# A windowed-attention plus mixture-of-experts kernel: weight loads moved earlier, conversions respaced, the last scatter halved

## The chip, the core and the metric

The kernel runs on one core of a Trainium2 chip. The metric is device time in microseconds (us) of one execution; several executions are timed, and one more is recorded by the hardware profiler. Engines are named as in the profile: PE (TensorE; PEld is its weight load), DVE (VectorE), ACT (ScalarE), POOL (GpSimd), SP (SyncE, which here only issues DMAs). A "q" behind a name (SPq, DVEq) is the engine's sequencer.

## The reference, cut to what matters

```python
# q, k, v: (8 batches, 8 heads, 576, 64); causal attention over a window of 64
scores = where(0 <= i - j < 64, q @ k.T / 8, -1e9)
x = (softmax(scores) @ v), heads joined          # (4608 tokens, 512)
do = x @ w_skip > 0
e = argmax(x @ w_gate); gate = softmax(x @ w_gate)[e]      # 8 experts
out = x;  out[do] = x + gate * (relu(x @ w1[e]) @ w2[e])   # w1: 512x1024, w2: 1024x512
```

## The kernel before

**First half, attention.** 36 tiles of 128 tokens are made in a software pipeline written out by hand: in step `t` the loop issues the loads of later steps (`at`), `score(t + 1)`, the gate products (`gate_at`), the softmax of tile `t` (`lessen`, `raise_e`), the output product of tile `t - 2` (`tile_out`, which calls `av_tile`), and the transposes of tile `t - 1`. Each engine runs its instructions in the order in which the code issues them, with semaphore waits between engines. `av_tile` writes the result of a tile to `x`, a pool of four buffers (`XPB`), and `store` sends it to `out`, at most three tiles behind. So tile 29 writes the buffer that the store of tile 25 must have left. All these loads and stores are issued by SP, one after the other, on SP's one queue.

**Routing, beside it.** POOL and DVE find each token's expert and its place in a list. After tile 21 POOL ranks the experts once (`close_first`) and writes `perm`, the row numbers of the first two experts' weights. SP reads `perm` into a register (L843, TENSOR_LOAD) before it can issue the first weight load. The lists of the last tiles are made after the attention, in generators that are stepped beside the first expert products (`late`, `later`, `side`).

**Second half, experts.** Ten items (an expert's tokens, up to 400) go through four quarters each. A quarter `k` is an up product of piece `(k, 0)` and, two quarters later, a down product of piece `(k - 2, 1)`. A piece is 128x1024 float32, 512 KB: loaded to a `raw` buffer (L845; the attention loop loads the first six, one at each step that `U0` names), then split for PE into `whi` (ACT, L854) and `wlo` (DVE, L858). `weights_to(n)` splits until `n` pieces are done; `expert_chunk` calls it ahead of each chunk of PE work and chooses `n`. Hidden activations are split likewise (`hh` on ACT L991, `hl` on DVE L994).

**The end.** An item's result `yo` is scattered to `out` by an indirect DMA that POOL issues (`give`, L1031). The last item has 112 rows, one token tile; its last quarter is made in two column halves, `z` = 0 and 1, each with its own DVE instruction (L1082). Behind it stands a conditional block for left-over tokens, skipped here: every engine loads the count `left` into a register (`left_over`, L1026) and branches (L1465). In the instruction streams the last DVE instruction (`z` = 1) and the last scatter stand behind that branch.

Of the kernel before, what the change touches and what calls it, by code (L numbers as in the profile page):

```python
# [11 lines left out]
I32 = mybir.dt.int32  # L12
AF = mybir.ActivationFunctionType
ALU = mybir.AluOpType
# [5 lines left out]
N, D, E, F = 4608, 512, 8, 1024  # L20
P = 128
# [31 lines left out]

NSLOW = 4
NRAW, NEARLY = 6, 2
U0 = (29, 30, 31, 32, 33, 34)
RATE = 1

BOTH = 20
# [7 lines left out]
PAIRED = 160  # L67
# [76 lines left out]
def window_attention_moe(ctx: ExitStack, tc, a, out):  # L144
    nc = tc.nc
# [570 lines left out]
    side, pace = [], [None]  # L716
# [14 lines left out]
    def rows_apart(ins):  # L731
        tc.declare_no_dep(ins.ins, group="rows", reason="every token is in one list entry: rows are disjoint")
        tc.add_to_no_dep_group("rows", ins.ins)
# [22 lines left out]
    OTHERS = [e for e in mybir.ALL_ENGINES if e != PE]  # L756

    GRP = [8, 8, 6, 6, 8]
    late = []

    later = []
# [48 lines left out]
    part = lambda k, w: (ITEMS[steps[k][0]][2], steps[k][1], w)  # L810
# [7 lines left out]
    when = {pc: n for n, pc in enumerate(pieces)}  # L818
# [16 lines left out]
    ptr = {"dma": 0, "split": 0, "free": 0, "use": 0}  # L835
# [13 lines left out]
    def weight_dma_first():  # L849
        weight_dma(ptr["dma"])  # L850
        ptr["dma"] += 1
# [10 lines left out]
    def weight_split(n):  # L862
        weight_hi(n)
        weight_lo(n, nc.vector)

    def weights_to(n):
        n = min(n, len(pieces), ptr["free"] + len(ring))
        while ptr["split"] < n:
            while ptr["dma"] < len(pieces) and idle:
                if not can_load(ptr["dma"]):  # L870
                    break
                weight_dma(ptr["dma"])
                ptr["dma"] += 1
            if ptr["dma"] == ptr["split"]:
                break
            weight_split(ptr["split"])
            ptr["split"] += 1
        while ptr["dma"] < len(pieces) and idle and can_load(ptr["dma"]):
            weight_dma(ptr["dma"])
            ptr["dma"] += 1  # L880
# [3 lines left out]
    def can_load(n):  # L884
        return pieces[n][0] % E < 2 or "order" in tables
# [139 lines left out]
    def left_over(engines):  # L1025
        return nc.values_load(tables["left"][0:1, 0:1], engines=engines, min_val=0, max_val=NSLOT)  # L1026

    counts = []

    def give(idx, yo):  # L1030
        ins = nc.gpsimd.indirect_dma_start(  # L1031
            out=out,
            out_offset=bass.IndirectOffsetOnAxis(ap=idx, axis=0),
            in_=yo,
            in_offset=None,
            bounds_check=N - 1,
            oob_is_err=False,
        )
        rows_apart(ins)
# [19 lines left out]
    def down(it, qi, wh, wl, tags="u"):  # L1059
        hh, hl = it.hh[qi], it.hl[qi]  # L1060
        if qi == 0:
            it.ys = []
            for tag in tags:
                for _ in range(1 if tag == "u" else 2):
                    pool = banks["v" if tag == "v" else "late"]
                    y = pool.tile([P, D], F32, name="y" + tag, tag=tag, bufs=1 if tag == "u" else 2)
                    it.ys.append(y)
        if it is its[-1]:
            m, ending_q = it.n, qi == NQ - 1
            halves = [(f, z) for f in range(2) for z in range(2)]  # L1070
            if ending_q:
                halves.sort(key=lambda fz: fz[1])
                yo = hpool["y"].tile([P, D], F32, name="yo", bufs=3)[:m]
            for f, z in halves:
                y = it.ys[z][:m, 0 : D // 2]
                w = slice(f * D + z * D // 2, f * D + (z + 1) * D // 2)
                mm3(y, hh[:, f], hl[:, f], wh[:, w], wl[:, w], qi == 0 and f == 0, ending_q and f == 1)
                if ending_q and f == 1:
                    if z == 1:
                        counts.append(left_over(OTHERS))  # L1080
                    c = slice(z * D // 2, (z + 1) * D // 2)
                    nc.vector.scalar_tensor_tensor(  # L1082
                        yo[:, c], y, it.gate[0], it.xg[0][:m, c], op0=ALU.mult, op1=ALU.add
                    )
                elif not ending_q and z == 1:
                    yield 0.65
            if ending_q:
                give(it.idx[0], yo)
            return
        for f in range(2):  # L1090
            w = slice(f * D, (f + 1) * D)
            first, last = qi == 0 and f == 0, qi == NQ - 1 and f == 1
            for j, y in enumerate(it.ys):
                m = it.rows[j]
                if it.small and j == it.nt - 1:
                    if f == 1:
                        down_small(it, qi, y, m)
                    continue
                r = slice(j * P, j * P + m)
                mm3(y[:m], hh[:, f, r], hl[:, f, r], wh[:, w], wl[:, w], first, last)  # L1100
            yield 0.65 * it.nt
        if qi == NQ - 1:

            def end():
                for j, y in enumerate(it.ys):
                    finish(y, it.xg[j], it.idx[j], it.gate[j], it.small and j == it.nt - 1)
                xfree.extend(it.xg)
                if it is its[-3]:
                    nc.gpsimd.drain()

            ending.append(end)
# [54 lines left out]
    with tc.manual_schedule():  # L1166
# [31 lines left out]
        for m in range(B // 2):  # L1198
            z = 2 * (m == 0)
# [9 lines left out]
        for t in range(NT - 1):  # L1209
            m, r = divmod(t, 9)  # L1210
# [37 lines left out]
            for f, n, j in lower_at.get(t, ()):  # L1248
                f(n, j)
            for _ in range(U0.count(t)):  # L1250
                weight_dma_first()
# [34 lines left out]
        place, turn = [0], [0, 0]  # L1286
# [4 lines left out]
        def expert_chunk():  # L1291
            k = place[0]
            last = len(steps) - 1
            if k != turn[0]:
                turn[:] = k, 0
            need = max(when[part(min(k + 1, last), 0)], when[part(min(k - 1, last), 1)] if k else 0) + 1
            most = ptr["free"] + min(RING, len(ring)) - 1
            it = its[steps[min(k, last)][0]]
            if late or later or side or P < it.n <= PAIRED:
                calm = k > 0 and turn[1] in ((1, 2) if k > 1 else (1,))  # L1300
                if turn[1] < 3:
                    need = max(when[part(min(k, last), 0)], when[part(k - 2, 1)] if k > 1 else 0) + 1
                weights_to(max(need, min(ptr["split"] + calm, most)))
            else:
                weights_to(max(need, min(ptr["split"] + RATE, most)))
            turn[1] += 1
            place[0], c = next(chunks)

        expert_chunk()
        drip()  # L1310
        tile_out(NT - 1)
# [12 lines left out]
        mr = moe.enter_context(tc.tile_pool(name="mr", bufs=1, side="right", reuse_waits="tile"))  # L1324
# [122 lines left out]
        while True:  # L1447
            k = place[0]
# [16 lines left out]
    with tc.If(more > 0):  # L1465
        with tc.For_i(0, more, 1) as i:
# [11 lines left out]
            it = Item(P)  # L1478
# [3 lines left out]
            for qi in range(NQ):  # L1482
                both = []
                for w in range(2):
                    n = 2 * qi + w
# [57 lines left out]
```

## Time and profile before

| | us |
|---|---|
| timed runs (3) | 402.59 to 403.35, median 402.61 |
| profiled execution, its own time | 404.55 |
| span of the profiled execution, first to last instruction | 402.8 |
| PE busy | 390.5 |
| DVE busy | 304.3 |
| mean granted TensorE clock | 0.995 of full speed |

The span is what the trace's times count from. The profiled execution took 1.94 us longer than the median of the timed ones, and 1.75 us lie around its span. Attention ends near 157 us; the lists are made until about 189 us; from there on PE runs expert products to 396.8 us.

### The profile page before, as it was taken

Reading aid. Unit: us, or ns where it says so; the run is one execution under the profiler, and the core shown is the slowest. Engines: PE = TensorE matmul, PEld = TensorE weight load, DVE = VectorE, ACT = ScalarE, POOL = GpSimd, SP = SyncE. Lnnn points to the kernel's source line nnn. Section 1 sums busy time; section 2 is a strip of 40 time slices with the busy share of each in tenths; the row PEclk is TensorE's granted clock in tenths of the full one; section 3 lists DMA queues with packets and bytes.
Section 4 is the critical chain, followed back from the end, with each engine's and each line's share of the span. In section 5 each row is a group of like instructions: output and inputs, shape, how many; then the busy total and the mean of one; then the engine's idle time right before and its main releaser. Section 6 shows DMA issues by size and latency. Waiting matters only on the chain.

```text
span 402.8 us, 11515 instructions
## 1 busy us (share of the span) xinstructions
PE 390.5 (97%) x4642; PEld 327.4 (81%) x4642; DVE 304.3 (76%) x538; ACT 218.1 (54%) x372; POOL 156.2 (39%) x276
## 2 busy tenths in 40 slices
PE   8999999999999999989999999999999999999994
PEld 3787778877787788878888888998888889988883
DVE  2888799899989898997758799465456485668981
ACT  1778776866876795554333554244335355444450
POOL 5121368157558688873605033032026030100410
PEclk9999999999999999999999999999999999999998
DMA  8999999999995887745705968645136787643420
GB/s 295 406 399 404 405 409 407 409 391 376 393 336 168 293 293 210 277 158 180 233 2 177 303 242 271 196 166 176 54 130 212 231 279 254 206 164 106 133 105 23
DMA packets 34600, 99.41 MB, mean 247 GB/s; under 512 B 4368, under 2 KB 5648, under 8 KB 34544
## 3 DMA queue, kind: packets, MB, share of 16 engines
q1 hardware_dynamic: 30480, 87.30, 61.5%
q0 software_dynamic: 3200, 9.58, 6.8%
q10 hardware_dynamic: 864, 1.77, 1.2%
q8 instruction: 37, 0.61, 0.6%
q14 instruction: 19, 0.16, 0.1%
HBM read 84.57 MB, written 14.39 MB: 246 GB/s over the span
## 4 chain that ended last, share of the span: by engine, by line
PE 59%; issue 14%; DVE 13%; DMA 7%; ACT 4%; POOL 2%; POOLq 0%; SPq 0%; DVEq 0%; ACTq 0%
PE av L388 7%; PE p L928 5%; PE pt L281 5%; PE p L930 5%; PE p L929 5%; PE ps L252 4%; DMA out<-yo,les 4%; DVE s L268 3%; PE yv L928 3%; PE yv L929 3%; PE yv L930 3%; DVE mx L267 2%; PE pw L331 2%; DMA raw<-wq 2%; PE ps L238 2%
## 5 line engine op out<-in xcount | busy, mean ns | idle before, releaser
L858 DVE TENSOR_TENSOR wlo<-raw,whi 128x1024 fp32r<-128x1024 f32 x70 | 85.6, 1237 | 13.5 <-ACT whi L854 11.7
L1031 POOL DMA_INDIRECT out<-yo,les x18 | 20.1, 1116 | 141.2 <-DVE yo L1022 132.4
L991 ACT ACTIVATE hh<-p 128x256 fp32r<-128x256 f32 (+4 forms) x56 | 22.9, 409 | 95.6 <-PE p L930 86.9
L854 ACT CAST whi<-raw 128x1024 fp32r<-128x1024 f32 x72 | 73.8, 1046 | 0.0
L928 PE MATMUL p<-xp,whi 128*128 128x256 f32 (+4 forms) x192 | 58.2, 303 | 0.2 <-ACT xp L902 0.2
L929 PE MATMUL p<-xp,whi 128*128 128x256 f32 (+4 forms) x192 | 57.1, 297 | 0.2 <-DVE xp L905 0.2
L994 DVE SCALAR_TENSOR_TENSOR hl<-p,hh 128x256 fp32r<-128x256 f32 (+4 forms) x56 | 25.0, 450 | 42.4 <-ACT hh L991 26.6
L930 PE MATMUL p<-xp,wlo 128*128 128x256 f32 (+4 forms) x192 | 56.9, 297 | 0.1
L273 ACT ACTIVATE s<-s 128x1024 f32<-128x1024 f32 x36 | 38.1, 1058 | 28.0 <-DVE s L268 27.6
L267 DVE TENSOR_REDUCE mx<-ps 128x8 f32<-128x1024 f32 x36 | 43.6, 1211 | 6.7 <-PE ps L252 6.7
L268 DVE TENSOR_TENSOR s<-ps,mx 128x1024 f32<-128x1024 f32 x36 | 44.1, 1225 | 4.6
L388 PEld LDWEIGHTS av<-vm,ptm 128*64 128x64 f32 x992 | 34.4, 136 | 8.9 <-issue 5.9
L388 PE MATMUL av<-vm,ptm 128*64 128x74 f32 x992 | 39.2, 230 | 0.1
L281 PE MATMUL pt<-gid,s 128*128 128x128 f32 x280 | 38.4, 279 | 0.1
L928 PEld LDWEIGHTS p<-xp,whi 128*128 128x128 f32 x192 | 36.2, 188 | 2.7 <-issue 0.6
L282 ACT COPY ptm<-pt 128x512 f32<-128x512 f32 x70 | 37.3, 581 | 1.2 <-PE pt L281 0.8
L929 PEld LDWEIGHTS p<-xp,whi 128*128 128x128 f32 x192 | 36.2, 188 | 1.2 <-DVE xp L905 0.5
L930 PEld LDWEIGHTS p<-xp,wlo 128*128 128x128 f32 x192 | 36.2, 188 | 0.3 <-DVE wlo L858 0.3
L252 PE MATMUL ps<-k,q 64*64 64x128 f32 x1024 | 33.4, 269 | 0.0
L281 PEld LDWEIGHTS pt<-gid,s 128*128 128x128 f32 x280 | 30.1, 141 | 3.1 <-issue 0.4
L353 POOL COPY vm<-vm 64x1184 f32<-64x1184 f32 (+1 forms) x17 | 18.8, 1108 | 35.4 <-ACT vm L351 23.8
L252 PEld LDWEIGHTS ps<-k,q 64*64 64x64 f32 x1024 | 30.2, 133 | 2.1
(241 smaller groups left out, 827.4 us busy)
## 6 DMA issues: line engine op xcount, KB each, us to landing
raw<-wq SPq DMA_DIRECT2D x72, 512.0 KB
vm<-vp SPq DMA_DIRECT2D x16, 592.0 KB
vT<-vT SPq DMA_DIRECT2D x16, 512.0 KB
out<-x SPq DMA_DIRECT2D x32, 256.0 KB
q<-qT SPq DMA_DIRECT2D x13, 512.0 KB
k<-kT SPq DMA_DIRECT2D x8, 640.0 KB
k<-kT SPq DMA_DIRECT2D x7, 512.0 KB
kt<-kT SPq DMA_DIRECT2D x8, 256.0 KB
```

The costliest lines, as they stand in the source:

```text
L252: nc.tensor.matmul(ps[64 * hf : 64 * hf + 64, r, p], q[h, p], k[h, :, p], start=False, stop=p == 3, skip_group_check=True,)
L267: nc.vector.tensor_reduce(mx, flat, axis=AX.X, op=ALU.max)
L268: pace[0] = nc.vector.tensor_tensor(s, flat, mx.unsqueeze(2).to_broadcast([P, 8, P]), op=ALU.subtract)
L273: nc.scalar.activation(s, s, AF.Exp, scale=0.125)
L281: nc.tensor.transpose(pt[:, p], s[:, 4 * r + p], ident)
L282: nc.scalar.copy(ptm[:, 4 * r : 4 * r + 4], pt)
L388: nc.tensor.matmul(av[64 * hf : 64 * hf + 64, h // 4, (h % 4) * VW : (h % 4 + 1) * VW], ptm[:, (h % 2) * 4 + h // 2, 64 * hf : 64 * hf + 6 ...
L854: nc.scalar.copy(ring[n % RING][0], raw_of[n])
L858: by.tensor_tensor(lo, raw_of[n], hi.bitcast(F32), op=ALU.subtract)
L928: nc.tensor.matmul(o, lh, rh, start=first, stop=False, skip_group_check=parts)
L929: nc.tensor.matmul(o, lh, rl, start=False, stop=False, skip_group_check=parts)
L930: nc.tensor.matmul(o, ll, rh, start=False, stop=last, skip_group_check=parts)
```

## The change

Four edits. `U0`: the six first weight pieces are issued at steps 28, 29, 30, 30, 31, 31 in place of 29 to 34. `expert_chunk`: while lists are made, a split is allowed at every second chunk, ahead of what is needed by one piece, and no further than the next need. `left_over` on the engines other than PE is called ahead of the last quarter's down product. The last result goes out in two scatters of half rows: `out` is seen as 9216 rows of 256, with indices `2 * idx + z` that two small DVE instructions write.

```diff
-U0 = (29, 30, 31, 32, 33, 34)
+U0 = (28, 29, 30, 30, 31, 31)
...
-    def give(idx, yo):
+    def give(idx, yo, parts=1):
         ins = nc.gpsimd.indirect_dma_start(
-            out=out,
+            out=out.rearrange("n (z c) -> (n z) c", z=parts),
...
+            if ending_q:
+                counts.append(left_over(OTHERS))
+                half = mr.tile([P, 2], I32, name="half")
+                for z in range(2):
+                    nc.vector.tensor_scalar(
+                        half[:m, z : z + 1], it.idx[0], 2.0, float(z), op0=ALU.mult, op1=ALU.add
+                    )
...
                 if ending_q and f == 1:
-                    if z == 1:
-                        counts.append(left_over(OTHERS))
                     c = slice(z * D // 2, (z + 1) * D // 2)
                     nc.vector.scalar_tensor_tensor(
                         yo[:, c], y, it.gate[0], it.xg[0][:m, c], op0=ALU.mult, op1=ALU.add
                     )
+                    give(half[:m, z : z + 1], yo[:, c], 2)
...
-            if ending_q:
-                give(it.idx[0], yo)
...
-            if late or later or side or P < it.n <= PAIRED:
-                calm = k > 0 and turn[1] in ((1, 2) if k > 1 else (1,))
-                if turn[1] < 3:
-                    need = max(when[part(min(k, last), 0)], when[part(k - 2, 1)] if k > 1 else 0) + 1
-                weights_to(max(need, min(ptr["split"] + calm, most)))
+            now = max(when[part(min(k, last), 0)], when[part(k - 2, 1)] if k > 1 else 0) + 1
+            if late or later or side:
+                calm = turn[1] % 2 == (0 if k > 1 else 1)
+                weights_to(max(now, min(need, ptr["split"] + calm)))
+            elif P < it.n <= PAIRED:
+                weights_to(max(now if turn[1] < 3 else need, min(ptr["split"] + (turn[1] in (1, 2)), most)))
```

How the order of instructions changes, at three places (`-` before, `+` after):

On SP, at attention steps 28 and 29: `vT`, `vm`, `vTt` and `vt` are the last value loads of the attention, `out<-x` is the store of tile 25, `raw` the weight pieces.

```order
 L211 DMA q<-qT 128x1024
 L426 DMA out<-x 128x512
+L843 TENSOR_LOAD perm
+L843 ISA x2
+L845 ISA
+L845 DMA raw_123<-wq 128x1024
 L292 DMA vT<-vT 128x1024
 L298 DMA vm<-vp 128x2x592
```

The register load of `perm` and the first weight piece now stand ahead of those four loads and that store; before they stood directly behind them. Two more pieces each now stand ahead of the loads of `kt` and `qt` (step 31) and of the store of tile 28 (step 32).

On DVE, in the stretch where the last lists are made (L604 is the one-hot table of the last tiles, L994 the low part of the hidden activations, L858 the low part of a weight piece):

```order
 L905 TENSOR_TENSOR xp_3348<-px_3518,xp_3348 128x4x128
-L994 SCALAR_TENSOR_TENSOR hl<-p_3525,hh 128x256
 L858 TENSOR_TENSOR wlo_3353<-raw_123,whi_3352 128x1024
+L994 SCALAR_TENSOR_TENSOR hl<-p_3528,hh 128x256
 L604 TENSOR_TENSOR xg_122<-cf,gk 128x1024
 L858 TENSOR_TENSOR wlo_3355<-raw_124,whi_3354 128x1024
 L994 SCALAR_TENSOR_TENSOR hl<-p_3578,hh 128x256
-L994 SCALAR_TENSOR_TENSOR hl<-p_3593,hh 128x256
 L858 TENSOR_TENSOR wlo_3357<-raw_125,whi_3356 128x1024
+L994 SCALAR_TENSOR_TENSOR hl<-p_3606,hh 128x256
```

A weight conversion now stands ahead of an `hl` where it stood behind it; ACT's `whi` and `hh` change places in the same way, and the number of conversions is the same.

On POOL, at the end of the program, of the change alone (`half` are the indices of the half rows; the ISA with eight waits closes the skipped block):

```order
L1026 TENSOR_LOAD left_4429 [waits DVE_49]
L1031 DMA out<-yo_5868,half_5865 9216x256 [waits DMASW3_49,DVE_49]
L1470 COMPARE_AND_BRANCH
...
L1470 ISA [waits DMASW4_49,DMASW5_49,DMASW3_49,DMASW6_49,DMASW2_49,DMASW7_49,DMASW1_49,DMASW0_49]
L1470 UNCONDITIONAL_BRANCH
L1031 DMA out<-yo_5868,half_5865 9216x256 [waits DMASW4_49,DVE_49]
```

The scatter of half 0 stands ahead of the branch and that of half 1 behind it; between them is the ISA that waits for the completion of POOL's own DMAs on all eight of their semaphores. It stood there before too, with both halves' one scatter behind it.

## Rows read from the trace of the kernel before

**Rows 1.** Page, parts 1, 2 (40 slices) and 5 (the conversions on ACT).

```profile
PE 390.5 (97%) x4642; PEld 327.4 (81%) x4642; DVE 304.3 (76%) x538; ACT 218.1 (54%) x372; POOL 156.2 (39%) x276
...
GB/s 295 406 399 404 405 409 407 409 391 376 393 336 168 293 293 210 277 158 180 233 2 177 303 242 271 196 166 176 54 130 212 231 279 254 206 164 106 133 105 23
...
L854 ACT CAST whi<-raw 128x1024 fp32r<-128x1024 f32 x72 | 73.8, 1046 | 0.0
```

**Rows 2.** Timeline of SP, 108 to 185 us: start, duration, issue.

```profile
116.54 0.34 SPq L426 DMA_DIRECT2D out<-x  x1
118.02 0.33 SPq L292 DMA_DIRECT2D vT<-vT  x1
...
123.40 0.38 SPq L426 DMA_DIRECT2D out<-x  x1
129.79 0.36 SPq L845 DMA_DIRECT2D raw<-wq  x1
130.26 0.91 SPq L428 DMA_DIRECT2D out<-x  x1
```

**Rows 3.** Timeline of POOL, 98 to 200 us: what writes perm.

```profile
128.53 0.23 POOL L653 TENSOR_SCALAR perm<-cm 128x2 int32<-128x2 f32 x1
```

**Rows 4.** Timeline of PE, 108 to 200 us: attention step 31.

```profile
133.52 0.64 PE L331 MATMUL pw<-vT,gid 128*32 128x256 f32 x8
```

**Rows 5.** Timeline of DVE, 108 to 200 us: x of tile 29.

```profile
136.34 0.69 DVE L401 TENSOR_TENSOR x<-av,r 128x512 f32<-128x512 f32 x1
```

**Rows 6.** Windows: busy time by engine, granted clock, DMA share, GB/s.

```profile
130.00:131.00 1.00, 1.00 (x30) 0.91 (x30) 0.87 (x2) 0.72 (x2) 0.94 (x2) 1.00 0.13 49
131.00:134.00 3.00, 3.00 (x64) 2.18 (x59) 2.80 (x7) 2.50 (x4) 2.66 (x5) 1.00 0.84 255
137.00:141.00 4.00, 4.00 (x90) 3.20 (x86) 3.80 (x10) 2.62 (x6) 2.78 (x12) 1.00 1.02 368
399.00:401.00 2.00, 0.00 (x0) 0.00 (x0) 0.00 (x0) 0.00 (x0) 0.12 (x1) 0.50 0.32 99
```

**Rows 7.** Timeline of PE, 176 to 200 us: its one long wait.

```profile
180.84 0.50 PE L929 MATMUL yw<-wlo,hh 128*128 128x512 f32 x1 [1.21 <-DVE wlo L858]
```

**Rows 8.** Timeline of DVE, 108 to 200 us: the work ahead of that wait.

```profile
175.16 1.22 DVE L858 TENSOR_TENSOR wlo<-raw,whi 128x1024 fp32r<-128x1024 f32 x1 [0.51 <-ACT whi L854]
176.30 2.28 DVE L604 TENSOR_TENSOR xg<-cf,gk 128x1024 bf16<-128x1024 f32 x1
178.50 2.27 DVE L858 TENSOR_TENSOR wlo<-raw,whi 128x1024 fp32r<-128x1024 f32 x1
```

**Rows 9.** Timelines of POOL and of ACT in the same stretch.

```profile
175.59 4.11 POOL L615 TENSOR_TENSOR xg<-xg,vals 128x640 bf16<-128x640 f32 x2
...
172.37 0.59 ACT L902 CAST xp<-px 128x512 fp32r<-128x512 f32 x1
...
174.08 1.99 ACT L854 CAST whi<-raw 128x1024 fp32r<-128x1024 f32 x2
```

**Rows 10.** Timeline of DVE, 372 us to the end.

```profile
396.09 0.48 DVE L1082 SCALAR_TENSOR_TENSOR yo<-yv,got,xg 112x256 f32<-112x256 f32 x1 [1.35 <-PE yv L930]
397.41 0.48 DVE L1082 SCALAR_TENSOR_TENSOR yo<-yv,got,xg 112x256 f32<-112x256 f32 x1 [0.84 <-DVEq L1465]
```

**Rows 11.** Timeline of POOL, 372 us to the end.

```profile
390.96 0.88 POOL L1031 DMA_INDIRECT out<-yo,les  x1 [0.34 <-DVE yo L1018]
398.17 0.94 POOL L1031 DMA_INDIRECT out<-yo,les  x1 [6.33 <-DVE yo L1082]
```

**Rows 12.** Lines L1026, L1465, L1540: count, ns min/median/max, first and last start.

```profile
L1026 DVEq TENSOR_LOAD <-left x1: 536/536/536, 396.1 to 396.1; - x1
L1465 POOLq EVENT_SEMAPHORE  x4: 17/43/1745, 391.8 to 393.7; - x4
L1540 SPq EVENT_SEMAPHORE  x14: 17/28/7156, 394.0 to 402.7; - x14
```

**Rows 13.** The chain that ended last, 392 us to the end.

```profile
394.19 3.75 issue
```

More of the change, by code (lines that the diff above doesn't have):

```diff
@@ L1035, in give @@
             in_offset=None,
-            bounds_check=N - 1,
+            bounds_check=parts * N - 1,
             oob_is_err=False,
```

## The prediction

> **What bounds the kernel now.** I read the page first: PE is busy for 97% of the span [rows 1], so time can be won only where PE waits, at the end behind its last product, or lost by making it wait. Then I read the timelines of the stretches that the order of instructions shows to be touched. Attention step 31 is tight: PE works without a break there, from the gate product of the last value load (133.52 us [rows 4]) into the output product of tile 29, and DVE writes that tile's `x` at 136.34 [rows 5]. SP's queue is late: after the store at 123.40 it issues nothing until 129.79, because the register load that comes next needs `perm`, which POOL writes at 128.53 to 128.76 [rows 2, 3]. In the stretch of the lists PE has one long wait, 1.21 us ahead of 180.84, for a `wlo` [rows 7]. At the end the last DVE instruction starts at 397.41, the last scatter at 398.17 [rows 10, 11], and the span closes at 402.8.
>
> **Weights sooner (`U0`).** This removes nothing: ACT's 72 conversions have 0.0 us of idle time before them [rows 1], none waits for a weight load, so an earlier load cannot speed up a conversion. It moves the wait. `perm` is made by an unchanged chain on POOL, so the register load still ends its wait at 128.76 and the first piece is still issued at 129.79. But now the loads `vT`, `vm`, `vTt`, `vt` and the store of tile 25, issued at 118.02 to 123.40 before [rows 2], stand behind it on SP. DMA lies idle meanwhile, and from 130.2 everything is in one line. SP's issues are 0.47 us apart (129.79 to 130.26), so the store of tile 25 is issued near 132.1, 8.7 us later than before.
>
> Who waits for that? PE needs `vT` at 133.52, and DVE needs tile 25's buffer for `x` of tile 29 at 136.34. Ahead of the store's end lie 512 KB of weights, 512 of `vT`, 592 of `vm`, 256 of `vTt`, 296 of `vt` and the store's own 256 (rows of float32 by the shapes): 2424 KB, 2.48 MB. Bytes begin to flow at about 131.0, 1.2 us after the issue, with 49 GB/s in the microsecond before; with a full queue the trace moves 368 GB/s (137 to 141), with a thin one 255 (131 to 134) [rows 6]. At 368 the line takes 6.7 us; the slow first microsecond costs about 0.3, and from last byte to the waiting engine I allow 0.6, since at the end bytes cease near 401.0 and SP's long wait of 7.156 us ends near 401.9 [rows 6, 12]. That is 138.6, 2.3 us after `x` wants to start. `vT` by the same sum (1.05 MB) is there at 134.8, 1.3 us late on PE; that lies inside the 2.3, not beside it, since `x` follows the product that follows the gate product. Later stores and `kt` come close to their due times under the shifted clock, without a margin, and I charge nothing more. Both ends: at the page's best slice, 409 GB/s [rows 1], with no receipt, the line ends at 137.1, 0.7 us late; at 255 GB/s at 140.7, 4.4 late. The full-queue row is the nearest one, so I take +2.3. PE and DVE are both almost full in attention (PE 4.00 and DVE 3.80 of 4 us [rows 6]), so the delay is not made good before its end.
>
> **Conversions.** The same instructions in another order; what is worth something is PE's 1.21 us. Before it DVE ran `hl`, `wlo` (175.16), the one-hot table L604 in 2.28 us and the next `wlo` in 2.27, where the `wlo` before took 1.22 [rows 8]. The slow two lie under two POOL instructions that took 4.11 us together [rows 9]: the engines held each other up, in turn. After the change `whi` goes ahead of the `hh` on ACT and starts near 172.9, behind the cast of 172.37 and 0.59 us, instead of 174.08 [rows 9], so this `wlo` runs near 174.0 to 175.2 and `hl` behind it. L604 can begin at 175.6 instead of 176.30. The worst case is the same alternation 0.3 us earlier: the second `wlo` ends at 180.5. If L604 gets in ahead of POOL's first, it ends near 179.3, before PE asks at 179.6. So the gain is 0.3 to 1.2; POOL is itself pushed back by the earlier `wlo`, which favours the second, and I take -1.0. The delayed `hl` costs nothing: the PSUM buffer that it frees is wanted by PE two products later, over 1 us off.
>
> **Register loads.** DVE loads `left` between the two halves, 0.536 us at 396.1 [rows 12], and the second half starts 0.84 us after the branch's wait begins [rows 10]. Moved ahead, the load lies in DVE's 1.35 us of idle time before 396.09, with the two index instructions of one column each, which I take well below the 0.48 us of a 256-column one. The second half then starts right behind PE's end at 396.8, 0.6 us sooner. This would be the gain if the scatter could follow at once.
>
> **Half-row scatters.** Half 0 is in SBUF at 396.57; POOL starts 0.28 us after the DVE instruction before (397.89 to 398.17), so at 396.85. The branch comes next, and behind it the instruction that waits for all of POOL's own DMAs. The trace has this sequence in little: the scatter at 390.96 (0.88 us), then a semaphore wait of 1.745 us until 393.7 [rows 11, 12], and POOL ready for the next scatter at 394.19 [rows 13], 3.23 us after the start. Before, this wait was over 4 us ahead of need. Now it stands between the halves: 396.85 + 3.23 = 400.1, against 398.17, so +1.9. The last transfer is half as large; its 2 us at 99 GB/s [rows 6] might shrink by up to 1.0, but POOL's share hardly depends on the size (0.88 us for 32 rows, 0.94 for 112), so I subtract 0.2. Net +1.7, with ends +0.9 (full halving) and +2.8 (the wait as long as from 398.17 to SP's release near 401.9, 3.7, and 0.4 to go on).
>
> The Trainium skill bears on this term: the page DMA: Bandwidth & Descriptors, section Anatomy of one DMA — SWDGE (gpsimd) path, gives each DMA from this path a fixed cost of about 2.0 us and bytes over 436 GB/s on top, which speaks against splitting one into two that follow each other. As an estimate by that page a half would take 2.3 us, and the end would be 0.7 us later than before, the whole 404.6; the row's 3.23 us stands in my sum, and 404.6 lies inside the forecast's own range.
>
> **The sum.** +2.3 - 1.0 + 1.7 = +3.0 us on the profiled execution's 404.55, so 407.6 there; the median of the timed runs is 1.94 us below that execution, so 405.6.
>
> **The rivals.** (a) Only the end costs: the store's bytes are not held by the loads in front, or something later had slack for 2 us. For it: no store's landing can be read in this trace. Against: one queue, and a full PE. Sum 402.61 - 1.0 + 1.7 = 403.3. (b) Only attention costs: the wait between the halves is short, since half 0 has fewer bytes, so the 0.6 us of the register load and some of the halving come through: 402.61 + 2.3 - 1.0 - 0.7 = 403.2. (c) Faster: the loads that were moved back arrive in time. It is decided by `x` of tile 29: if the store of tile 25 lands by 136.3, which needs over 460 GB/s from 131.0 or a queue that lets it pass, attention costs nothing, and the conversions' 1.2 with an end of at most +0.9 give 402.3; without the POOL wait, 400.7. (d) Worse: the sparse rate of 255 GB/s rules and `x` of tiles 31 and 32, behind four more pieces, waits too: +4.4 + 2.0 - 0.3 + 1.7 = 410.4. (e) PE's stop lets the granted clock fall: at the end it fell to 0.50, 1.2 GHz, about 2 us after the last product; a stall of over 2 us might touch this, and PE's work would take up to twice as long while it lasts. It shares (d)'s chance.
>
> **How the numbers follow.** Forecast 0.62; (a) 0.09; (b) 0.09; (c) 0.10; (d) and (e) 0.10. The forecast's own ends are 403.5 and 408.0. I set the range at 403.0 to 408.0: it leaves out (c), (d) and (e). A measurement of this kernel can tell about 0.2%, 0.8 us, from no change, so slower begins at 403.4. The forecast and (d), (e) are slower, and nearly half of (a) and (b), which stand at its edge: 0.80. Same: the rest of these and a little of (c): 0.11. Faster: the rest of (c), and (b) where the end gives more: 0.09.
>
> **What would show it.** In the trace after: SP idle from about 117 to 129.8; `vT` issued near 130.3; no bytes for about 9 us ahead of 131; a wait for a DMA on PE's gate product or DVE's `x` near 134 to 139; attention ending some 2 us later; PE's wait near 181 below 0.9 us; two scatters at the end 3 us or more apart, the second starting over 5 us before the span's end. Wrong would be: `perm` ready before 120, no gap at `x` of tile 29, or a second scatter within 1.5 us of the first.

## The result, and the profile after

The changed kernel takes 408.20 us (median of 6 runs, 407.28 to 409.05) where the kernel before takes 402.60 (6 runs, 401.87 to 403.35): a ratio of 1.0140 [1.0122, 1.0158], 5.6 us slower. The forecast said slower by 3.0 us, with 408.0 as the upper end of its range; the direction is right, and the size is just outside.

The page of the profiled execution first: shares of the span, then GB/s in 40 slices.

```profile
span 406.9 us, 11519 instructions
PE 390.2 (96%) x4642; PEld 327.8 (81%) x4642; DVE 303.4 (75%) x540; ACT 217.7 (54%) x372; POOL 160.9 (40%) x277
GB/s 295 409 397 381 406 409 392 394 407 351 400 309 11 346 360 178 296 231 158 226 21 169 307 239 285 187 172 157 83 125 207 261 264 217 240 160 70 190 38 23
```

PE's busy time is that of [rows 1] within 0.3 us, so no work was added to it: the 4.1 us by which the span grew are, but for some products at a slower clock (below), time in which PE waits. The slice with 11 GB/s is the new hole in the transfers, 122 to 132 us, where [rows 1] has 168.

SP's timeline in that hole (start, duration, issue) answers to [rows 2]:

```profile
117.40 0.34 SPq L426 DMA_DIRECT2D out<-x  x1
130.66 0.36 SPq L845 DMA_DIRECT2D raw<-wq  x1
131.12 1.18 SPq L292 DMA_DIRECT2D vT<-vT  x1
132.47 0.39 SPq L298 DMA_DIRECT2D vm<-vp  x1
132.91 0.46 SPq L314 DMA_DIRECT2D vTt<-vTt  x1
133.47 0.43 SPq L315 DMA_DIRECT2D vt<-vpt  x1
134.00 0.82 SPq L426 DMA_DIRECT2D out<-x  x1
```

As forecast, SP does nothing until `perm` lets it load its register, and the value loads and the store of tile 25 come out behind the first weight piece. This execution runs 0.85 us late already at step 31, ahead of anything that the change touches there (its score products start at 133.16 instead of 132.31), and all that is compared below is compared with that taken off. The timelines of PE and of DVE in step 31, to be read beside [rows 4, 5]:

```profile
133.40 1.04 PE L252 MATMUL ps<-k,q 64*64 64x128 f32 x32
137.44 1.08 PE L331 MATMUL pw<-vT,gid 128*32 128x256 f32 x8 [3.00 <-DMA vT<-vT]
138.46 2.24 PE L388 MATMUL av<-vm,ptm 128*64 128x74 f32 x32
141.30 0.17 DVE L399 TENSOR_SCALAR r<-av 128x8 f32<-128x8 f32 x1 [5.29 <-PE av L560]
141.74 0.69 DVE L401 TENSOR_TENSOR x<-av,r 128x512 f32<-128x512 f32 x1
```

PE stands for 3.00 us for `vT`, not for 1.3, and DVE, ahead of `x` of tile 29, waits for PE and not for the store. Then the gate product takes 1.08 us instead of 0.64, and the output product 2.24 instead of the 1.25 that it takes elsewhere in the trace. The windows say why: the column ahead of the last two (DMA share, GB/s) is the granted clock.

```profile
131.00:132.00 1.00, 1.00 (x33) 1.00 (x32) 0.92 (x1) 0.58 (x2) 0.94 (x2) 1.00 0.20 45
132.00:133.00 1.00, 1.00 (x16) 0.91 (x10) 0.93 (x4) 0.66 (x1) 0.92 (x2) 1.00 0.80 266
133.00:134.00 1.00, 1.00 (x31) 0.77 (x32) 1.00 (x3) 1.00 (x3) 0.85 (x2) 1.00 0.82 274
134.00:135.00 1.00, 0.45 (x19) 0.20 (x8) 0.87 (x2) 0.97 (x2) 0.90 (x2) 1.00 0.95 323
135.00:136.00 1.00, 0.00 (x0) 0.00 (x0) 1.00 (x1) 0.06 (x1) 0.55 (x1) 1.00 0.96 288
136.00:137.00 1.00, 0.00 (x0) 0.00 (x0) 0.02 (x1) 0.00 (x0) 0.00 (x0) 1.00 0.95 290
137.00:138.00 1.00, 0.56 (x8) 0.23 (x8) 0.00 (x0) 0.00 (x0) 0.00 (x0) 0.68 0.93 327
138.00:140.00 2.00, 2.00 (x34) 1.54 (x27) 0.00 (x0) 1.39 (x2) 0.00 (x0) 0.50 1.05 393
140.00:141.00 1.00, 1.00 (x17) 0.85 (x14) 0.00 (x0) 0.04 (x1) 0.00 (x0) 0.62 1.01 385
141.00:142.00 1.00, 1.00 (x12) 0.90 (x9) 0.63 (x3) 0.26 (x1) 0.00 (x0) 1.00 1.06 422
```

After the 3 us of rest the clock is 0.50, 1.2 GHz, for some 3 us. The wait and the longer products (3.00 + 0.44 + 0.99) are 4.43 of the 4.54 us by which steps 31 to 34 grew (from the start of the score products of 31 to that of 34: 149.89 - 133.16 = 16.73, before 144.50 - 132.31 = 12.19).

In the stretch of the lists, DVE's rows that answer to [rows 8]:

```profile
177.91 1.23 DVE L858 TENSOR_TENSOR wlo<-raw,whi 128x1024 fp32r<-128x1024 f32 x1 [0.25 <-ACT whi L854]
179.05 0.42 DVE L994 SCALAR_TENSOR_TENSOR hl<-p,hh 128x256 fp32r<-128x256 f32 x1
179.39 1.22 DVE L604 TENSOR_TENSOR xg<-cf,gk 128x1024 bf16<-128x1024 f32 x1
180.52 1.22 DVE L858 TENSOR_TENSOR wlo<-raw,whi 128x1024 fp32r<-128x1024 f32 x1
```

L604 and the `wlo` behind it take 1.22 us each instead of 2.28 and 2.27, and PE's 1.21 us of [rows 7] are gone. (POOL's long pair, 3.46 us, now starts at 183.25 and slows two later `wlo`, for which PE does not wait.) At the end, DVE's two halves and the two scatters on POOL, for [rows 10, 11]:

```profile
398.13 0.48 DVE L1087 SCALAR_TENSOR_TENSOR yo<-yv,got,xg 112x256 f32<-112x256 f32 x1 [0.90 <-PE yv L930]
398.84 0.48 DVE L1087 SCALAR_TENSOR_TENSOR yo<-yv,got,xg 112x256 f32<-112x256 f32 x1 [0.23 <-PE yv L930]
```

```profile
398.89 0.94 POOL L1031 DMA_INDIRECT out<-yo,half  x1 [5.01 <-DVEq L1470]
402.82 0.94 POOL L1031 DMA_INDIRECT out<-yo,half  x1 [2.98 <-DMA out<-yo,les]
```

Between its halves DVE now waits 0.23 us for PE, where it waited 0.84 on the branch; the first scatter starts 0.37 us after the start of PE's last product (398.52), and the second 3.93 us behind it. The releaser in the row bears the name of the scatters of whole rows, but the last of those had started at 393.00; the DMA whose bytes still move in this wait (99 GB/s from 400 to 401 us) is the first half, so it is the landing of the first half that the second waits for.

The two profiled executions differ by 4.1 us (408.68 and 404.55), the medians by 5.6, because the profiled execution of before was 1.94 us above its median and that of after 0.48 above its own. By place, after against before in the traces: +0.85 ahead of step 31, +4.54 in steps 31 to 34, +0.09 to the output product of tile 34 (the last but one), -2.87 from there to the first product into `yv` (40.85 to 37.98), -0.57 in the experts, +2.06 behind the start of PE's last product (6.32 to 8.38); the sum is 4.1.

### The profile page after: what moved, and what is told of

It reads as the page before. It is cut to its first block, busy times and chain, and to the rows that moved or that the text cites. A ratio compares the mean times of both kernels' runs of the same rounds, so it can differ in the third digit from the quotient of the medians.

```text
span 406.9 us, 11519 instructions
## 1 busy us (share of the span) xinstructions
PE 390.2 (96%) x4642; PEld 327.8 (81%) x4642; DVE 303.4 (75%) x540; ACT 217.7 (54%) x372; POOL 160.9 (40%) x277
## 4 chain that ended last, share of the span: by engine, by line
PE 49%; issue 18%; DMA 14%; POOL 12%; DVE 4%; ACT 1%; POOLq 1%; SPq 0%; DVEq 0%; ACTq 0%
PE av L388 7%; DMA out<-yo,les 5%; PE p L928 4%; PE p L930 4%; PE p L929 4%; PE pt L281 4%; DMA vT<-vT 4%; PE ps L252 4%; DMA vm<-vp 2%; PE yv L928 2%; PE yv L929 2%; PE yv L930 2%; PE pw L331 2%; POOL out L1031 2%; PE yw L928 2%
## 5 line engine op out<-in xcount | busy, mean ns | idle before, releaser
L858 DVE TENSOR_TENSOR wlo<-raw,whi 128x1024 fp32r<-128x1024 f32 x70 | 86.4, 1246 | 13.4 <-ACT whi L854 13.0
L1031 POOL DMA_INDIRECT out<-yo,les x17 | 19.2, 1128 | 133.4 <-DVE yo L1022 130.9
L994 DVE SCALAR_TENSOR_TENSOR hl<-p,hh 128x256 fp32r<-128x256 f32 (+4 forms) x56 | 25.1, 450 | 42.0 <-ACT hh L991 30.3
```

The lines of the kernel that those rows point to most:

```text
L858: by.tensor_tensor(lo, raw_of[n], hi.bitcast(F32), op=ALU.subtract)
```

## The experiments

Each kernel was timed in five rounds against the kernel before on its own chip: the first four (median of before 403.13), the next four (402.85) and the last four (406.13) on one chip each. Microseconds of different chips are not subtracted here, and ratios of different chips only with care: the one kernel that was timed on two of these chips, conv_reg below, gave two ratios whose intervals don't overlap.

**undo_u0 and u0_only: how much is the weight loads' step?**

```diff
 undo_u0, against after
-U0 = (28, 29, 30, 30, 31, 31)
+U0 = (29, 30, 31, 32, 33, 34)
 u0_only, against before
-U0 = (29, 30, 31, 32, 33, 34)
+U0 = (28, 29, 30, 30, 31, 31)
```

> The changed kernel with the weight loads back at steps 29 to 34. Theory A (the register wait ahead of the last value loads cost 3.0 us of PE waiting for vT and about 1.5 us of slow clock behind it): 408.2 - 4.5 = 403.7, no DMA wait on the gate product of step 31, granted clock 1.00 throughout. Rival B (the loads themselves, not the wait, or something later, cost it): at least 406.5.

> The kernel before with only the six weight loads moved sooner. Theory A: 402.6 + 4.5 = 407.1, PE waits about 3 us for vT, the clock falls to 0.50 for 3 to 4 us. Theory as predicted (the store of tile 25 is what counts, +2.3): 404.9.

undo_u0: 404.18, ratio 1.0028 [1.0013, 1.0043]. u0_only: 407.12, ratio 1.0114 [1.0084, 1.0143]. The two add up to the whole (1.14% and 0.28% against 1.40%). So the attention term is 4.6 us [3.4, 5.8], where the forecast had 2.3; the rest of the change is +1.1 us [0.5, 1.7], where it had -1.0 + 1.7 = +0.7. Only the first is off.

The total of u0_only is the one that its theory A named, but its profiled execution (405.87, one of its two fastest) does not show the way there: PE waits 2.16 us, the clock stays at 1.00, and it is DVE that waits last, for the store.

```profile
136.27 0.64 PE L331 MATMUL pw<-vT,gid 128*32 128x256 f32 x8 [2.16 <-DMA vT<-vT]
140.36 0.69 DVE L401 TENSOR_TENSOR x<-av,r 128x512 f32<-128x512 f32 x1 [1.31 <-DMA out<-x]
```

Steps 31 to 34 take 15.51 us there, 3.3 more than before.

**u0_step29: which of the six pieces?** All of the changed kernel, with only the first piece back at step 29.

```diff
-U0 = (28, 29, 30, 30, 31, 31)
+U0 = (29, 29, 30, 30, 31, 31)
```

> The changed kernel with the weight loads at steps 29, 29, 30, 30, 31, 31: as many pieces sooner, but the first stands behind the value loads of step 29 as before. Theory A (only the first piece's register wait matters): within 0.7 us of the kernel with all loads put back (403.7), no wait for vT. Rival B (six pieces in a crowd delay kt, qt and the stores): 405 or more, with waits for kt or for x.

404.40, ratio 1.0035 [1.0020, 1.0050], and steps 31 to 34 take 12.19 us again, to the hundredth what they take before. Five pieces that come sooner cost nothing; what costs is the first piece and its register load ahead of the value loads. The next run parts these two.

**perm_wait_only: the register load without the bytes.** The kernel before; only the register load that waits for `perm` stands at step 28. No weight byte moves.

```diff
+    def row_first():
+        e = pieces[0][0]
+        wrow[e] = nc.values_load(perm[0:1, e % E : e % E + 1], engines=[SP], min_val=0, max_val=(E - 1) * NQ * P)
...
+            if t == 28:
+                row_first()
             for _ in range(U0.count(t)):
                 weight_dma_first()
```

> The kernel before, with only the register load of perm moved to step 28, ahead of the value loads; all weight loads stay where they were, so vT is the first transfer after the wait. Theory A with the wait alone: vT lands 1.3 us (512 KB) sooner than with a weight piece ahead of it, so PE waits about 1.7 us and the clock may hold: 402.6 + 2 = 404.6. If the weight piece ahead is what delays vT, no wait and 402.6. If the idle DMA's slow start is what counts, still 3 us and 407.

406.06, ratio 1.0073 [1.0051, 1.0095]. Its PE and DVE in step 31:

```profile
134.07 0.64 PE L331 MATMUL pw<-vT,gid 128*32 128x256 f32 x8
140.10 0.69 DVE L401 TENSOR_TENSOR x<-av,r 128x512 f32<-128x512 f32 x1 [3.24 <-DMA out<-x]
```

`vT`, now the first transfer behind the wait, is there in time, and DVE waits 3.24 us for the store of tile 25 to give its buffer free. This is the forecast's mechanism by itself: the wait in SP's queue makes the store late, without a byte of weights. None of the three cases in the expectation foresaw it: all went by `vT`. By the ratio it costs 2.9 us [2.1, 3.8], so the register load alone is most of the 4.6; that the piece behind it adds the rest is likely, but the two intervals overlap.

**vt_alone: is `vT` late because of the bytes behind it?** The loads `vm`, `vTt` and `vt` go ahead of the register load, and pieces 2 to 6 to step 31; then only the first piece stands ahead of `vT`, and small stores and loads behind it.

```diff
-U0 = (28, 29, 30, 30, 31, 31)
+U0 = (28, 31, 31, 31, 31, 31)
...
-                when_at(first_of[n] - AHEADV, load_v, n)
+                when_at(first_of[n] - AHEADV, load_v if n < 15 else load_vT, n)
...
-            when_at(9 * m + 2, load_v_tail, m)
+            when_at(9 * m + 2 - (m == 3), load_v_tail, m)
...
+        when_at(28, load_vm, 15)
```

> The changed kernel with the loads vm, vTt and vt of step 29 issued ahead of the register load, and the weight pieces 2 to 6 at step 31: the first piece stands ahead of vT as it does after the change, and behind vT only the store of tile 25, two half stores and four small loads. Theory A (vT is late because the bytes issued behind it share its rate: by its end 1.64 MB had moved, where raw and vT are 1.05 MB): vT lands near 135.5, PE waits for it 1.3 us or less where it waited 3.0, the granted clock stays at 1.00, and x of tile 29 hardly waits for the store; the whole is 404.5 to 405.5. Theory B (vT is late by its own start: an issue of 1.18 us and a queue that was empty): PE still waits 2.2 us or more, and the whole is 407 to 408.

409.44, ratio 1.0079 [1.0054, 1.0104]. SP's issues, PE's wait and the windows from 132 to 136 us:

```profile
130.19 0.36 SPq L845 DMA_DIRECT2D raw<-wq  x1
130.60 0.91 SPq L292 DMA_DIRECT2D vT<-vT  x1
131.62 0.37 SPq L426 DMA_DIRECT2D out<-x  x1
```

```profile
136.53 0.64 PE L331 MATMUL pw<-vT,gid 128*32 128x256 f32 x8 [2.59 <-DMA vT<-vT]
```

```profile
132.00:133.00 1.00, 1.00 (x15) 0.76 (x17) 0.97 (x4) 1.00 (x2) 0.92 (x2) 1.00 1.17 221
133.00:134.00 1.00, 0.94 (x36) 0.70 (x28) 1.00 (x2) 0.97 (x3) 0.74 (x4) 1.00 0.78 143
134.00:135.00 1.00, 0.00 (x0) 0.00 (x0) 0.87 (x2) 0.56 (x1) 1.00 (x1) 1.00 0.88 293
135.00:136.00 1.00, 0.00 (x0) 0.00 (x0) 0.51 (x1) 0.00 (x0) 0.10 (x1) 1.00 1.02 395
```

PE still waits 2.59 us: theory B by its wait, though the ratio lies between the two. From the issue of the first piece to the end of PE's wait it is 6.34 us, against 6.78 after (137.44 - 130.66), and 5.91 to 6.92 in u0_only, undo_half, half_ahead and u0_filled, which have all the bytes behind. So an effect of the bytes behind is not shown. What this does cure is the store: `x` of tile 29 has no wait of its own, the clock stays at 1.00, and steps 31 to 34 take 14.85 us, the 12.19 of before and PE's wait.

**u0_filled: what does the fall of the clock cost?** The changed kernel with 24 products of 256 columns ahead of the gate product of step 31, into the tile that it then overwrites; no output depends on them.

```diff
+        for _ in range(fill):
+            nc.tensor.matmul(
+                pw[:, : nt * P], onesb, onesb.unsqueeze(1).to_broadcast([P, nt, P]),
+                start=True, stop=True, skip_group_check=True,
+            )
...
-        vws[n] = gate(vTs.pop(n), 2)
+        vws[n] = gate(vTs.pop(n), 2, 24 if n == 15 else 0)
```

> The changed kernel with 24 products of 512 columns in bf16 on PE ahead of the gate product of step 31, into the same PSUM tile, which the gate product then writes over: PE works through the wait for vT (24 are worth more than the 3.0 us). Theory A (the fall of the granted clock to 0.50 at 137 to 141 costs some 1.5 us of the attention term): the clock stays at 1.00 there, pw takes 0.64 us and the output product 1.25 us again, steps 31 to 34 take 15.0 to 15.5 us where they took 16.73, and the whole is 406.5 to 407.0; should the fill outlast the wait, as much more as it does. Theory B (x of tile 29 or a later load would have held PE just as long): steps 31 to 34 take 16.2 us or more with a clock of 1.00, and the whole stays at 408.

409.95, ratio 1.0086 [1.0054, 1.0119]. (The width in the expectation was a slip; the first row has the shape.)

```profile
134.13 2.79 PE L331 MATMUL pw<-onesb 128*128 128x256 bf16 x24
137.37 0.64 PE L336 MATMUL pw<-vT,gid 128*32 128x256 f32 x8 [0.45 <-DMA vT<-vT]
137.94 1.26 PE L393 MATMUL av<-vm,ptm 128*64 128x74 f32 x32
```

```profile
141.04 0.69 DVE L406 TENSOR_TENSOR x<-av,r 128x512 f32<-128x512 f32 x1 [0.88 <-DMA out<-x]
```

With PE at work the clock stays at 1.00 in every window from 130 to 142 us, and `pw` and `av` take 0.64 and 1.26 us again. But what PE gains, DVE then waits for: the store of tile 25 holds `x` of tile 29 for 0.88 us, and steps 31 to 34 still take 16.09 us. Between these two traces the fall of the clock is worth 0.6 us (16.73 - 16.09), not the 1.4 that it adds to the products; the rest lies beside the store's landing. The bound that I had given theory B was 16.2; the wait that it named is there, and A's sum is not.

The price in the timed runs stays open. The same steps take 15.51 and 16.26 us in the traces of u0_only and undo_half, where the clock holds too, so single traces differ by as much. In u0_only's timed runs the three with a mean granted clock of 0.996 or 0.997 took 405.68 to 406.63, the three with 0.991 to 0.994 took 407.60 to 409.21; after has 0.994 or less in all six. This hints at more than 0.6 us, but perm_wait_only's times do not follow its clock in this way. The ratio of u0_filled lies below that of after, 1.0086 against 1.0140, but after was not timed beside it on this chip.

**undo_half and half_ahead: what do the half scatters cost?** undo_half is the changed kernel with one scatter of whole rows at the end. half_ahead keeps both, but POOL's register load comes behind the second, so that both stand ahead of the branch and of the instruction that waits for POOL's own transfers.

```diff
 undo_half, against after
-                    give(half[:m, z : z + 1], yo[:, c], 2)
...
+            if ending_q:
+                give(it.idx[0], yo)
 half_ahead, against after
-    OTHERS = [e for e in mybir.ALL_ENGINES if e != PE]
+    OTHERS = [e for e in mybir.ALL_ENGINES if e not in (PE, POOL)]
...
-        counts.append(left_over([PE]))
+        counts.append(left_over([PE, POOL]))
```

> The changed kernel with one scatter of whole rows at the end; register loads stay early. Theory A (POOL's wait for its own DMAs between the halves costs 2 us, and the early register load gives 0.6 once the wait is gone): 408.2 - 2.6 = 405.6, last scatter about 1.4 us behind PE's last product. Rival (the end's cost is the second scatter's own 0.94 us): 407.3.

> The changed kernel with POOL's register load put behind the second scatter, so that both scatters and the second DVE half stand ahead of the branch, and nothing waits between the halves. Theory A: second scatter at most 1.0 us behind the first, 408.2 - 2.6 - up to 0.5 for the smaller last transfer = 405.1 to 405.6. Rival (two indirect DMAs cost their fixed time in any order): 407 or more.

undo_half: 405.16, ratio 1.0053 [1.0030, 1.0076]. half_ahead: 406.07, ratio 1.0071 [1.0044, 1.0098]. The last scatters of undo_half, and then those of half_ahead:

```profile
398.80 0.95 POOL L1031 DMA_INDIRECT out<-yo,les  x1 [5.71 <-DVE yo L1082]
```

```profile
399.45 0.95 POOL L1031 DMA_INDIRECT out<-yo,half  x1 [5.01 <-DVE yo L1087]
400.71 0.94 POOL L1031 DMA_INDIRECT out<-yo,half  x1 [0.30 <-issue]
```

undo_half is what its theory A said; half_ahead lies between its two, with a second scatter 1.26 us behind the first. From the start of PE's last product to the end of the span it is 6.32 us before, 5.68 in undo_half, 8.38 after and 6.32 in half_ahead. So the early register load gives 0.64 us, the half scatters take 2.70, and of these 2.06 are the wait that stands between them. Even without it halves show no gain: the span of half_ahead (405.4) closes 4.69 us after its second scatter starts, that of undo_half (403.4) 4.60 after its only one, and the second start is later. That does not say that half the bytes land no sooner: in half_ahead the first half's transfer runs beside, and the instructions that close the block (POOL, 403.3 to 403.6 us) come behind the last scatter. In after, where the last half is alone and behind the branch, it is 4.08 us from its start to the span's end, against 4.63 before.

**conv_only, conv_reg and conv_reg_again: the parts that remain.** conv_only is the kernel before with the order of the conversions of the change; conv_reg adds the early register loads, with one whole scatter; conv_reg_again is conv_reg on the third chip.

```diff
 conv_only, against before
-            if late or later or side or P < it.n <= PAIRED:
...
+            now = max(when[part(min(k, last), 0)], when[part(k - 2, 1)] if k > 1 else 0) + 1
+            if late or later or side:
 conv_reg, against conv_only
             m, ending_q = it.n, qi == NQ - 1
+            if ending_q:
+                counts.append(left_over(OTHERS))
...
-                    if z == 1:
-                        counts.append(left_over(OTHERS))
```

> The kernel before with only the conversions respaced. Theory A (PE's 1.2 us wait for a wlo goes, and part of the wait was DVE and POOL blocking each other): 401.2 to 401.6. Rival (the 2.8 us that the changed kernel regained between 142 and 195 us all come from this edit): 399.8. Rival (regained only because attention came late): 402.4 or more.

> The kernel before with the conversions respaced and the register loads early, one scatter, weight loads as before. Theory A: the two gains add, 402.6 - 1.2 - 0.6 = 400.8, which beats both kernels. Rival (the register load's 0.6 us is not on the path): same as the conversions alone.

> The kernel before with the conversions and the early register loads of the change, the old weight loads and one scatter, once more, since 0.9974 [0.9953, 0.9996] was near the edge of what a measurement can tell. Theory A (the conversions give 0.9 us and the register load 0.6 us): 401.2 to 402.0, ratio 0.9965 to 0.9985. Theory B (the first look was scatter of the measurement): ratio 0.9990 to 1.0010.

conv_only: 402.78, ratio 0.9989 [0.9963, 1.0014], not told apart from no change; the interval holds its theory A (0.9965 to 0.9975) as well as the rival that nothing is regained. conv_reg: 402.08, ratio 0.9974 [0.9953, 0.9996]. conv_reg_again: 403.18, ratio 0.9929 [0.9906, 0.9952], more than its theory A asked for. This kernel beats the kernel before by 0.3% on one chip and by 0.7% on the other, and with it the changed one. The two intervals don't overlap, and why the third chip gives more is not settled.

**before_again: was the wait of [rows 7] an exception?** The kernel before once more, without an edit.

> The kernel before, unchanged. Theory A (the 40.85 us from the last output product of attention to the first product of the lists' end, and with it 2 us of the profiled execution's 404.55, were that execution's own): this profile has 38.5 to 39.0 us there, a wait of PE of about 0.4 us for wlo near 180, and an execution near 402.6. Theory B (the kernel before holds them in every execution): 40.5 us or more again, with the wait of 1.2 us, and the conversions are worth 2 us or more.

405.88, ratio 0.9999 [0.9973, 1.0026]. PE's waits from 150 to 200 us:

```profile
PE yw L929 <- DVE wlo L858: 1.2, 1, 1.2
PE av L388 <- ACT ptm L282: 0.5, 1, 0.5
```

The wait is there again, and from the output product of tile 34 to the first product into `yv` it takes 40.76 us (40.85 in the first profile). Theory A falls: this was not that one execution's own. Yet u0_only and perm_wait_only, with the same old conversions, take 38.82 and 38.69 there, with a wait of 0.4 us, and the ten executions with the new ones 37.75 to 38.65, with no wait for a `wlo`. So the old order is open to a wait that depends on how DVE and POOL meet; the new one was never caught in it. (u0_only and perm_wait_only come to this stretch some 4 us later than before, so they are no plain repeats of it.)

## Why the forecast was right in direction and short in size

**What bounds the kernel** was read rightly. PE's work did not change, and each part was worth what it did to a wait.

**The mechanism in attention** was right: SP idle to 130.7, `vT` and the store of tile 25 behind the register load, the store's landing as the last wait on DVE. perm_wait_only shows it by itself, and with all of `U0`'s change it is there in u0_only (1.31 us), undo_half (1.18), half_ahead (0.33) and u0_filled (0.88). In the trace of after alone it is hidden: there PE's wait for `vT` and the slower clock behind it ended last. **The step that failed is the size of this term**, +2.3 us, in the sentence "The full-queue row is the nearest one, so I take +2.3". It measured 4.5 in the trace of after and 4.6 by the ratios; in u0_only, u0_filled and undo_half, where the clock holds and the store ends last, `x` of tile 29 comes 3.50, 4.09 and 4.25 us later than before, counted from the start of step 31. The store by itself landed 3.7 us after `x` could have started, and two pieces of the sum were off, by 0.8 and 0.6 us. The 0.8 that are left up to 4.5 are PE's path, which the forecast had put inside the store's.

- The line moved more slowly than the full-queue row. The forecast took 368 GB/s from [rows 6], measured with the queue long in flow. After, from 132.0 (45 GB/s in the microsecond before) to 139.7 the windows above add up to the 2.44 MB that were left up to the store's end, 317 GB/s; the same working gives 326 in u0_only, 310 in undo_half and 294 in perm_wait_only. That is between the two rows of the same group, 368 and 255. My other end, 4.4 us late at 255 GB/s with no landing, came near the measured 4.5 by luck: its rate was too low, and the landing was missing.
- A transfer is not landed when the bytes in front of it and its own have moved. I allowed 0.6 us. In the stretch from 130 to 138 us the trace after gives these times from issue to landing:

```profile
raw<-wq SPq DMA_DIRECT2D x3, 512.0 KB, 5.8
...
out<-x SPq DMA_DIRECT2D x1, 256.0 KB, 6.9
```

The store issued at 134.00 landed near 140.9, 1.2 us after the bytes in its line were through (1.1, 1.5 and 2.0 us in u0_only, undo_half and perm_wait_only). `vT` needs 1.05 MB with the piece ahead; by the end of PE's wait 1.64 MB had moved. The Trainium skill, page DMA: Bandwidth & Descriptors, section Queues, rings and completion order, says that a later descriptor of such a queue may finish its write before an earlier one, since data descriptors carry no barrier. No run here shows it: the 0.6 MB from behind in those 1.64 are also what moves while `vT` lands 2.0 us after its bytes, and vt_alone, with small transfers in their place, kept its wait. What the runs do show is the piece ahead of it: `vT` takes 3.3 us from issue to landing in perm_wait_only, without that piece, and 5.3, 6.2 and 5.7 in u0_only, undo_half and half_ahead, with it.

**`vT` as a wait of PE** was put at 1.3 us and called no cost of its own, since it "lies inside the 2.3". That last part held wherever the store ended last: in u0_filled, with 0.45 us of it left, `x` of tile 29 comes 8.12 us after step 31 starts, and after 8.58. It failed by 0.8 us in the trace of after. The size, 2.2 to 3.0 us in five executions, was off for the reasons above, and with it came the fall of the clock. **Rival (e)** had named that fall ("a stall of over 2 us might touch this") and shared 0.10 with (d). It is in the profiled execution of after, where it costs 0.6 us net against u0_filled, and in half_ahead's, where the clock is 1.00 until PE has worked for a microsecond behind a wait of 2.51 us, then 0.63 (139 to 140 us) and 0.50 (to 142). It is not in undo_half's, with a wait of 3.03 us and a clock of 1.00 from 132 to 141 us, nor in those of u0_only and vt_alone (2.16 and 2.59 us). So in the traces it explains neither the 2.3 us that were missing nor every execution. PE's rows of half_ahead, where the output product takes 1.79 us instead of 1.25:

```profile
138.16 0.64 PE L331 MATMUL pw<-vT,gid 128*32 128x256 f32 x8 [2.51 <-DMA vT<-vT]
138.73 1.79 PE L388 MATMUL av<-vm,ptm 128*64 128x74 f32 x32
```

**Conversions**, -1.0 (0.3 to 1.2): PE's wait is gone, in the way the forecast described (L604 unhindered, from 179.39). Its value against the kernel before is 2.9 us in the traces of the lists, 0.9 against the two executions of old conversions with a shorter wait, and 0.4 in the timed runs of conv_only, an interval from a gain of 1.5 to a loss of 0.6. The traces flatter it: the profiled execution of before lies 1.9 us above its median, that of conv_only (401.50) 1.3 below its own. My figure lies inside what can be told, and is not confirmed.

**Register loads**, 0.6 us sooner: 0.64 in undo_half. **Half scatters**, net +1.7 with ends 0.9 and 2.8: +2.06 in the trace. The wait between the starts is 3.93 us, not the 3.23 of the earlier scatter of 32 rows; the shrinking of the last transfer is 0.5 (4.08 us from its start to the span's end, 4.63 before), not 0.2. Both errors are small and partly cancel. The Trainium skill, page DMA: Bandwidth & Descriptors, section Anatomy of one DMA — SWDGE (gpsimd) path, gives a DMA of this path a fixed cost of about 2.0 us, from which the forecast had estimated 2.3 us for a half. This case's trace has 3.93 from start to start, 0.94 of the instruction itself and 2.98 until the landing of the first lets the second go, and the measurement decides.

**The other rivals.** (a), only the end costs, and (c), the loads arrive in time, fell with u0_only; (b), only attention costs, fell with undo_half. (d) wanted 410.4 and the sparse rate; the rate was above it, and the second wait, `x` of tiles 31 and 32 behind four more pieces, is 0.27 us at most in the trace after (0.5 in undo_half, 1.23 in u0_filled, where (d) had 2.0). u0_step29 shows that these pieces cost nothing where the queue is not late.

**The range** was too narrow for its own terms: 402.61 with each term at its slow end, +4.4 - 0.3 + 2.8, is 409.5, and the range stopped at 408.0. The measured 408.20 lies inside the terms' ends.

**Open** are why the transfers move 266 to 323 GB/s for five microseconds after the hole with a full queue, and 385 to 422 afterwards; what the fall of the clock costs in the timed runs; and why the two chips disagree on conv_reg.

## What to carry to other kernels

When a load moves to an earlier place in an in-order queue, look first at what its address waits for: here one register load held five innocent transfers for 10 to 12 us, and five pieces moved sooner behind those transfers were free. Price a transfer that someone waits for from issue to landing, not by bytes over the best rate, and where two rows for a rate lie far apart, carry both to the end of the sum and let the range hold both. A last transfer cut in two is two transfers: ask what stands between their starts, and how much sooner half the bytes can land.

## What the runs showed that I had not expected

- A 3.00 us rest of PE in mid-kernel was followed by a clock of 0.50 for some 3 us in one execution (after), and a rest of 2.51 us by such a fall in another (half_ahead); rests of 3.03 (undo_half) and 2.59 us (vt_alone) were followed by none. The length of the rest alone does not decide it.
- Half as many bytes in a scatter of 112 rows saved little: 4.08 us from start to the end of the span in after, against 4.63 for whole rows before, and nothing in half_ahead (4.69, against 4.60 in undo_half).
- The second issue on SP behind the pause is slow: 1.18 us for `vT` after, 1.11 in undo_half, 0.91 in vt_alone, and 0.91 for the store at 130.26 before, where `vT` in the flowing queue took 0.33 [rows 2].
